# A retention layer and two MLPs: the split of w_out kept in DRAM, attention state in two tiles, and other warm-up matmuls

## The chip, the cores and the metric

The kernel runs on one core of a Trainium2 chip. The metric is the device time of one execution in microseconds, from its start to its end on that core. The profiled execution is one more run, taken with the hardware profiler; the span is the time from its first to its last instruction.

## The reference

Retention attention (a causal mask that decays with distance) over 8 sequences of 576 positions with 8 heads of 64, then two MLPs on the 4608 tokens. Activations are float32, the four weights are float64.

```python
Dmat = np.where(rel >= 0, gamma[:, None, None] ** rel[None, :, :], 0.0)
ret = scale * np.matmul(q, k.transpose(0, 1, 3, 2)) * Dmat[None]
x = np.matmul(ret, v)                     # 4608 tokens x 512
h = x @ moe_w_in                          # 512 x 2048
x = (h * (1.0 / (1.0 + np.exp(-1.702 * h)))) @ moe_w_out
h = x @ moe2_w_in
out = (h - np.tanh(h)) @ moe2_w_out
```

## The kernel before

**Tiles and steps.** The 4608 tokens are nine blocks of 512, the 2048 hidden units 16 slices f of 128. The main loop runs over steps s = (j, f), 288 in all: j = 0 to 8 are the nine blocks of the first MLP (MLP1), j = 9 to 17 the same blocks for the second (MLP2). A step has 12 matmuls of `mm_in(s)` (hidden slice f from `xh`, `xl` and `wi`) and 12 of `mm_out(s - 2)` (the slice of two steps before goes through `wos` into the four accumulators `acc`). Every float32 operand is split into a high part (rounded to fp32r, an ACT copy) and a low part (the rest, a subtraction), and three of the four products are summed; that makes 12 matmuls out of 4.

**Between the two products.** `act_a(s)` makes the nonlinearity. In MLP1 it is a tanh on ACT (L382) and one DVE operation (L383). In MLP2 it is tanh, square and another square on ACT (L387 to L389), then on DVE L390, L392, L393, L394 (a comparison that writes the mask) and L395 (the masked copy of a polynomial for small values). `act_b(s)`, which stands at the front of the next step, splits the result: `g` high on ACT (L400), `g` low on DVE (L401).

**w_out.** `wo` lies in SBUF as float32, one tile of 256 KB per f. In every step `split_wo` makes the two parts anew: ACT copies the high one (L187), POOL subtracts for the low one (L188). It stands behind `act_a(s)` in the code and works for `mm_out(s - 1)`, one step ahead of its use. For the second MLP the decoded `w_out` goes to DRAM (L134) and comes back in block j=8.

**w_in.** It is split once, when it is decoded: `wi` stays in SBUF. The second MLP's goes to DRAM (`w2s`, written from POOL's queue at L148) and is loaded back in j=8, also from POOL's queue.

**The decoder.** The float64 weights come in 64 chunks of 512 KB (`stg`, L93). A chunk takes DVE operations L103, L106, L111 and L117, an ACT operation (L105) and a multiplication on POOL (L126), in three pieces; `dec_c` then splits it (L142, L143). `dec_slot` runs three pieces: twice per step in j=0, and in every third step of j = 1 to 7.

**Attention.** 72 batches (36 tiles of 128 positions, two halves bt of the heads), one in every second step of j < 8. It makes the input of the MLP1 block one block ahead. `sbd` and `s_sb` hold the running state of all heads in one tile each; PE reads `sbd` at L246, DVE updates `s_sb` at L297. The loads of a tile (`at`, 1 MB, L207) wait for PE's last use of the buffer.

**MLP2's input.** The first MLP's result goes to DRAM block by block and comes back as `x2s`; `x2_split` copies its high part on ACT (L446) and subtracts for the low one on POOL (L447), in steps f = 6, 8, 10 and 12.

**Start.** Before the first attention batch stand 22 matmuls on zeros (L488). The order on each engine is the order of the code: scheduling is by hand, and each engine takes its instructions one after the other. DMAs that SP issues form one queue, those of POOL another.

Of the kernel before, what the change touches and what calls it, by code (L numbers as in the profile page):

```python
# [36 lines left out]
CA = C1 / (2 * C2)  # L37
CB = C0 / C2 - CA * CA
S_MAX = 0.0625
N_WARM = 22  # L40


@with_exitstack
def kernel(
# [32 lines left out]
    gt_sb = const.tile([P, HP], F32, name="gt_sb")  # L77
    ebias = const.tile([P, 1], F32, name="ebias")
    abias = const.tile([P, 1], F32, name="abias")
    sbd = const.tile([P, HP, P], F32, name="sbd")  # L80
    s_sb = const.tile([P, HP, HD], F32, name="s_sb")


    win = {}
    wout = {}
    w2_d = {}
    wo2_d = {}
    stg = {}
    half = {}

# [24 lines left out]
    def dec_b(m, f, c):  # L115
        hi, _, e, z = half[m, f, c]
        nc.vector.scalar_tensor_tensor(  # L117
            out=e, in0=hi, scalar=-(2 ** 31), in1=e, op0=ALU.bitwise_and, op1=ALU.bitwise_or
        )
        del stg[m, f, c]  # L120
        if c == 1 and m == 0:
            o = wts.tile([P, DM], F32, tag=f"wo{f}", name="wo")
            wout[f] = o
        else:
            o = z.bitcast(F32)
        nc.gpsimd.tensor_tensor(out=o, in0=z.bitcast(F32), in1=e.bitcast(F32), op=ALU.mult)  # L126
        half[m, f, c] = o

    def dec_c(m, f, c):
        o = half.pop((m, f, c))  # L130
        if c == 1:
            if m == 1:
                d = dram.tile([P, DM], F32, tag=f"wo2{f}", name="wo2")
                nc.sync.dma_start(out=d, in_=o)  # L134
                wo2_d[f] = d
            return
        if m == 0:
            s = wts.tile([P, 2, KD, P], F32R, tag=f"wi{f}", name="wi")
        else:
            s = st_p.tile([P, 2, KD, P], F32R, tag="stg", name="w2s", bufs=3)  # L140
        sv = s.rearrange("p a k c -> p a (k c)")
        nc.scalar.activation(out=sv[:, 0], in_=o, func=ACTF.Copy)  # L142
        nc.gpsimd.tensor_tensor(out=sv[:, 1], in0=o, in1=sv[:, 0].bitcast(F32), op=ALU.subtract)  # L143
        if m == 0:
            win[f] = s
        else:
            d = dram.tile([P, 2, KD, P], F32R, tag=f"w2{f}", name="w2")
            nc.gpsimd.dma_start(out=d, in_=s)  # L148
            w2_d[f] = d


    chunks = []
# [26 lines left out]
        for _ in range(3):  # L179
            dec_piece()  # L180

    wos = {}

    def split_wo(s):
        j, f = divmod(s, NF)
        t = t_p.tile([P, 2, DM], F32R, tag="wos", name="wos")
        nc.scalar.activation(out=t[:, 0], in_=wout[f], func=ACTF.Copy)  # L187
        nc.gpsimd.tensor_tensor(out=t[:, 1], in0=wout[f], in1=t[:, 0].bitcast(F32), op=ALU.subtract)  # L188
        wos[s] = t


    at = {}
# [42 lines left out]
    def result_of(ps):  # L235
        return ps[:, 1, 2 * P:4 * P].rearrange("p (k c) -> p k c", k=2)

    def bat_sq(b):

        t, bt = divmod(b, BPT)  # L240
        if t % TPS == 0:
            return False
        n = HD if t % TPS == 4 else P
        for k in range(2):
            hp = 2 * bt + k
            nc.tensor.matmul(  # L246
                result_of(pa[b])[:, k, 0:n], lhsT=sbd[:, hp], rhs=at[t][:, 0, hp * P:hp * P + n],
                start=k == 0, stop=False, skip_group_check=True,
            )
        return True  # L250
# [29 lines left out]
    def bat_p(b):  # L280
        t, bt = divmod(b, BPT)
        ps, p = pa[b], pt[b]
        nc.vector.tensor_tensor(
            out=p.rearrange("p i k c -> p i (k c)"), in0=ps[:, :, 0:2 * P],
            in1=mt_sb[:, bt].rearrange("p i k c -> p i (k c)"), op=ALU.mult,
        )
        if t % TPS == 4:
            nc.vector.memset(p[0:HD, :, :, HD:P], 0.0)
        if t % TPS == TPS - 1:
            return  # L290
        state = state_of(ps)
        if t % TPS in (0, 4):
            nc.vector.tensor_copy(out=s_sb[:, 2 * bt:2 * bt + 2], in_=state)
            return
        for k in range(2):
            hp = 2 * bt + k
            nc.vector.scalar_tensor_tensor(  # L297
                out=s_sb[:, hp], in0=s_sb[:, hp], scalar=gt_sb[:, hp:hp + 1], in1=state[:, k],
                op0=ALU.mult, op1=ALU.add,
            )  # L300

# [14 lines left out]
    def bat_x(b):  # L316
        t, bt = divmod(b, BPT)
        j, tl = divmod(t, TPB)
        x = result_of(pa.pop(b))
        if b % BPB == 0:  # L320
            xh[j] = x_p.tile([P, KD, BLK], F32R, tag="xh", name="xh")
            xl[j] = x_p.tile([P, KD, BLK], F32R, tag="xl", name="xl")
        c = slice(tl * P, (tl + 1) * P)
        hps_ = slice(2 * bt, 2 * bt + 2)
        nc.scalar.activation(out=xh[j][:, hps_, c], in_=x, func=ACTF.Copy)  # L325
        nc.vector.tensor_tensor(  # L326
            out=xl[j][:, hps_, c], in0=x, in1=xh[j][:, hps_, c].bitcast(F32), op=ALU.subtract
        )
        if t % TPS == TPS - 1:
            return  # L330
        for i in range(2):
            r = halves(i)
            nc.scalar.activation(out=sbd[r, hps_, r], in_=s_sb[r, hps_], func=ACTF.Copy)

    def attn_step(b, ps=None):

# [117 lines left out]
    def w2_load_out(f):  # L454
        t = wts.tile([P, DM], F32, tag=f"wo{f}", name="wo")
        nc.sync.dma_start(out=t, in_=wo2_d[f])
        wout[f] = t
# [12 lines left out]
    nc.vector.memset(sbd, 0.0)  # L470
# [28 lines left out]
    n_steps = 2 * NB * NF  # L499
    for s in range(n_steps + LAG):  # L500
        j, f = divmod(s, NF)
        so = s - LAG + 1
        if s >= n_steps and so < n_steps:
            split_wo(so)
        if 0 < s <= n_steps:
            act_b(s - 1)
        if j == 0:
# [78 lines left out]
```

## Time and profile before

| | us |
|---|---|
| median of three runs | 1818.05 |
| lowest and highest run | 1816.42, 1819.49 |
| the profiled execution | 1820.6 |
| its span | 1818.8 |

| engine | busy us | share of the span |
|---|---|---|
| PE (matmuls) | 1760.5 | 97% |
| PEld (weight loads) | 1428.1 | 79% |
| DVE | 1252.0 | 69% |
| ACT | 838.3 | 46% |
| POOL | 672.0 | 37% |

The mean granted clock of TensorE is 0.986 of the full one. The shares are averages over stages that differ: the start with the first nine attention batches (to 41.47 us), block j=0 with the densest decoding (to about 206), the other blocks of MLP1 with attention (to 916.72), block j=8 without attention (to 1003.76), and MLP2. The timeline names an instruction by start, duration, engine, line, tile written and tiles read; a bracket at its end tells how long the engine was idle before it and what it waited for. PEld is the weight load of a matmul. A group of several like instructions in a row is one line with their count.

### The profile page before, as it was taken

What the parts mean: (1) busy time and instruction counts of PE and PEld (TensorE: products, weight loads), DVE (VectorE), ACT (ScalarE), POOL (GpSimd) and SP (SyncE); (2) the same over time, 40 slices, a digit from 0 to 9 for tenths busy, and PEclk for the clock granted to TensorE, in tenths of its full rate; (3) what the DMA queues carried; (4) which work ended last, traced back from release to release, by engine and by line L of the source; (5) the groups of instructions that cost most, each with busy time, mean ns of one, the idle gap of its engine ahead of it and who ended that gap; (6) DMA issues with size and microseconds to landing.
All of it is one profiled execution on the core that took longest, in us unless ns stands there. A gap on an engine that the chain in (4) does not pass through costs nothing.

```text
span 1818.8 us, 22935 instructions
## 1 busy us (share of the span) xinstructions
PE 1760.5 (97%) x8918; PEld 1428.1 (79%) x8918; DVE 1252.0 (69%) x1689; ACT 838.3 (46%) x1555; POOL 672.0 (37%) x527
## 2 busy tenths in 40 slices
PE   7788899999999999999999999999999999999998
PEld 5556788888888888888888878787878787878787
DVE  6999756566565565633333687888887878788877
ACT  2444434334343434434333555555555555555554
POOL 4666544434344344432234232323232323232322
PEclk7999999999999999999999999999999999999999
DMA  5344323123222322211044201010101010101000
GB/s 216 117 138 151 133 87 103 72 99 125 90 98 88 122 87 95 86 53 70 1 145 143 84 1 47 1 47 1 47 1 47 1 47 1 46 1 47 1 23 24
DMA packets 36254, 126.61 MB, mean 70 GB/s; under 512 B 4400, under 2 KB 4528, under 8 KB 30512
## 3 DMA queue, kind: packets, MB, share of 16 engines
q1 hardware_dynamic: 30960, 108.28, 17.2%
q0 software_dynamic: 4608, 16.78, 2.6%
q8 instruction: 70, 1.15, 0.3%
q14 instruction: 40, 0.33, 0.1%
q10 hardware_dynamic: 576, 0.08, 0.0%
HBM read 93.67 MB, written 31.46 MB: 69 GB/s over the span
## 4 chain that ended last, share of the span: by engine, by line
PE 46%; DVE 32%; ACT 19%; issue 2%; POOL 1%; DMA 0%; SPq 0%; DVEq 0%; POOLq 0%; ACTq 0%
PE acc L414 20%; PE h L373 19%; DVE t L395 8%; DVE sq L394 6%; ACT pl L389 6%; DVE pl L392 6%; DVE pl L393 5%; ACT g L400 5%; ACT sq L388 4%; ACT t L387 4%; DVE z L106 2%; PE pat L260 2%; PE pat L311 1%; DVE e L117 1%; DVE g L401 1%
## 5 line engine op out<-in xcount | busy, mean ns | idle before, releaser
L373 PE MATMUL h<-xh,wi 128*128 128x512 f32 x2304 | 762.4, 392 | 11.2 <-POOL wi L143 6.1
L188 POOL TENSOR_TENSOR wos<-wo,wos 128x512 fp32r<-128x512 f32 x288 | 373.2, 1296 | 1034.8 <-ACT wos L187 1025.9
L373 PEld LDWEIGHTS h<-xh,wi 128*128 128x128 f32 x2304 | 434.6, 189 | 109.0 <-POOL wi L143 10.1
L414 PE MATMUL acc<-g,wos 128*128 128x512 f32 x1728 | 434.7, 400 | 20.4 <-ACT wos L187 11.5
L373 PE MATMUL h<-xl,wi 128*128 128x512 f32 x1152 | 450.3, 391 | 0.0
L416 PE MATMUL acc<-wos,g 128*128 128x512 f32 x1728 | 424.7, 392 | 12.1 <-POOL wos L188 12.1
L401 DVE TENSOR_TENSOR g<-t,g 128x512 fp32r<-128x512 f32 x288 | 289.3, 1005 | 194.8 <-ACT g L400 189.2
L414 PEld LDWEIGHTS acc<-g,wos 128*128 128x128 f32 x1728 | 324.1, 191 | 102.0 <-ACT wos L187 14.5
L416 PEld LDWEIGHTS acc<-wos,g 128*128 128x128 f32 x1728 | 321.7, 188 | 91.9 <-POOL wos L188 24.5
L400 ACT ACTIVATE g<-t 128x512 fp32r<-128x512 f32 x288 | 181.3, 630 | 388.3 <-DVE t L395 353.8
L373 PEld LDWEIGHTS h<-xl,wi 128*128 128x128 f32 x1152 | 217.5, 189 | 45.0
L383 DVE SCALAR_TENSOR_TENSOR t<-t,h 128x512 f32<-128x512 f32 x144 | 98.2, 682 | 139.6 <-ACT t L382 139.3
L187 ACT ACTIVATE wos<-wo 128x512 fp32r<-128x512 f32 x288 | 178.9, 621 | 1.6 <-PE acc L416 0.3
L382 ACT ACTIVATE t<-h 128x512 f32<-128x512 f32 x144 | 85.8, 596 | 162.7 <-PE h L373 161.4
L395 DVE COPY_PREDICATED t<-sq,pl 128x512 f32<-128x512 int32 x144 | 141.0, 979 | 5.0
L390 DVE TENSOR_TENSOR t<-h,t 128x512 f32<-128x512 f32 x144 | 99.7, 692 | 44.0 <-ACT sq L388 44.0
L325 ACT ACTIVATE xh<-pat 128x256 fp32r<-128x256 f32 x64 | 24.5, 382 | 225.2 <-PE pat L311 225.2
L326 DVE TENSOR_TENSOR xl<-pat,xh 128x256 fp32r<-128x256 f32 x64 | 27.0, 422 | 145.6 <-ACT xh L325 145.6
L394 DVE TENSOR_SCALAR sq<-sq 128x512 int32<-128x512 f32 x144 | 116.6, 810 | 0.0
L389 ACT ACTIVATE pl<-sq,abias 128x512 f32<-128x512 f32 x144 | 104.4, 725 | 4.7
L392 DVE SCALAR_TENSOR_TENSOR pl<-pl,sq 128x512 f32<-128x512 f32 x144 | 99.7, 693 | 9.5
L393 DVE SCALAR_TENSOR_TENSOR pl<-pl,h 128x512 f32<-128x512 f32 x144 | 98.9, 687 | 4.9
(61 smaller groups left out, 1286.0 us busy)
## 6 DMA issues: line engine op xcount, KB each, us to landing
at<-in_attn_dram SPq DMA_DIRECT2D x35, 1024.0 KB, 5.5
stg<-in_w_dram SPq DMA_DIRECT2D x64, 512.0 KB, 4.3
x<-o SPq DMA_DIRECT2D x36, 256.0 KB, 2.7
x2s<-x SPq DMA_DIRECT2D x9, 1024.0 KB, 5.5
out_dram<-o SPq DMA_DIRECT2D x36, 256.0 KB, 2.2
w<-w2s POOLq DMA_DIRECT2D x16, 512.0 KB, 3.1
wi<-w POOLq DMA_DIRECT2D x16, 512.0 KB, 4.1
wo<-z SPq DMA_DIRECT2D x16, 256.0 KB, 5.7
```

The lines of the kernel that those rows point to most:

```text
L187: nc.scalar.activation(out=t[:, 0], in_=wout[f], func=ACTF.Copy)
L188: nc.gpsimd.tensor_tensor(out=t[:, 1], in0=wout[f], in1=t[:, 0].bitcast(F32), op=ALU.subtract)
L373: nc.tensor.matmul(h, lhsT=win[f][:, a, k], rhs=xs[b][:, k], start=(n == 0), stop=(n == 3 * KD - 1))
L389: nc.scalar.activation(out=pl, in_=sq, func=ACTF.Square, bias=abias)
L392: nc.vector.scalar_tensor_tensor(out=pl, in0=pl, scalar=CB, in1=sq, op0=ALU.add, op1=ALU.mult)
L393: nc.vector.scalar_tensor_tensor(out=pl, in0=pl, scalar=C2, in1=h, op0=ALU.mult, op1=ALU.mult)
L394: nc.vector.tensor_scalar(sq.bitcast(I32), sq, S_MAX, None, ALU.is_lt)
L395: nc.vector.copy_predicated(out=t, mask=sq.bitcast(I32), data=pl)
L400: nc.scalar.activation(out=g[:, 0], in_=t, func=ACTF.Copy)
L401: nc.vector.tensor_tensor(out=g[:, 1], in0=t, in1=g[:, 0].bitcast(F32), op=ALU.subtract)
L414: nc.tensor.matmul(acc[m], lhsT=wo[:, a, c], rhs=g[:, b], start=first, stop=last)
L416: nc.tensor.matmul(acc[m], lhsT=g[:, a, c], rhs=wo[:, b], start=first, stop=last)
```

## The change

**w_out.** `split_wo` is gone. `dec_c` splits a decoded `w_out` chunk as it splits `w_in`: an ACT copy (L139 of the new file) and a POOL subtraction (L140) into a tile with both parts, 512 KB, which is written to DRAM (`wd`, L143) from SP's queue. In j=0 the same tile serves `mm_out` directly. From j=1 on `wo_load(s)` (L180) loads the two parts from DRAM in every step, on SP's queue, for use two steps later; the pool `wos` has four buffers. The float32 `wo` tiles, their write to DRAM for the second MLP and the 16 loads in j=8 go.

**w_in of the second MLP.** Its write and its loads move from POOL's queue to SP's.

**sbd, s_sb.** One tile per bt instead of one for both.

**Warm-up.** 12 matmuls of 512 columns in bf16 and 12 of 256 columns in fp32r on four weight slices, in place of 22 of 256 columns in bf16. A second zero tile is set on POOL.

```diff
-N_WARM = 22
+N_WARM = 12
...
+    wos_p = ctx.enter_context(tc.tile_pool(name="wos", bufs=4))
...
-    sbd = const.tile([P, HP, P], F32, name="sbd")
-    s_sb = const.tile([P, HP, HD], F32, name="s_sb")
+    sbd = [const.tile([P, 2, P], F32, name=f"sbd{bt}") for bt in range(BPT)]
+    s_sb = [const.tile([P, 2, HD], F32, name=f"s_sb{bt}") for bt in range(BPT)]
...
-        if c == 1 and m == 0:
-            o = wts.tile([P, DM], F32, tag=f"wo{f}", name="wo")
-            wout[f] = o
-        else:
-            o = z.bitcast(F32)
+        o = z.bitcast(F32)
...
         if c == 1:
-            if m == 1:
-                d = dram.tile([P, DM], F32, tag=f"wo2{f}", name="wo2")
-                nc.sync.dma_start(out=d, in_=o)
-                wo2_d[f] = d
-            return
-        if m == 0:
+            if m == 0:
+                s = wos[f] = wos_p.tile([P, 2, DM], F32R, tag="wos", name="wos")
+            else:
+                s = st_p.tile([P, 2, DM], F32R, tag="stg", name="w2s", bufs=3)
+        elif m == 0:
             s = wts.tile([P, 2, KD, P], F32R, tag=f"wi{f}", name="wi")
+            win[f] = s
         else:
             s = st_p.tile([P, 2, KD, P], F32R, tag="stg", name="w2s", bufs=3)
-        sv = s.rearrange("p a k c -> p a (k c)")
+        sv = s if c == 1 else s.rearrange("p a k c -> p a (k c)")
         nc.scalar.activation(out=sv[:, 0], in_=o, func=ACTF.Copy)
         nc.gpsimd.tensor_tensor(out=sv[:, 1], in0=o, in1=sv[:, 0].bitcast(F32), op=ALU.subtract)
-        if m == 0:
-            win[f] = s
-        else:
-            d = dram.tile([P, 2, KD, P], F32R, tag=f"w2{f}", name="w2")
-            nc.gpsimd.dma_start(out=d, in_=s)
-            w2_d[f] = d
+        if c == 1 or m == 1:
+            d = dram.tile([P, 2 * DM], F32, tag=f"w{m}{f}{c}", name="wd")
+            nc.sync.dma_start(out=d, in_=sv.rearrange("p a n -> p (a n)").bitcast(F32))
+            (wo_d if c else w2_d)[m, f] = d
...
-    def split_wo(s):
+    def wo_load(s):
         j, f = divmod(s, NF)
-        t = t_p.tile([P, 2, DM], F32R, tag="wos", name="wos")
-        nc.scalar.activation(out=t[:, 0], in_=wout[f], func=ACTF.Copy)
-        nc.gpsimd.tensor_tensor(out=t[:, 1], in0=wout[f], in1=t[:, 0].bitcast(F32), op=ALU.subtract)
-        wos[s] = t
+        t = wos[s] = wos_p.tile([P, 2, DM], F32R, tag="wos", name="wos")
+        nc.sync.dma_start(out=t.rearrange("p a n -> p (a n)").bitcast(F32), in_=wo_d[int(j >= NB), f])
...
-    def w2_load_in(f):
+    def w2_load(f):
         t = wts.tile([P, 2, KD, P], F32R, tag=f"wi{f}", name="wi")
-        nc.gpsimd.dma_start(out=t, in_=w2_d[f])
+        nc.sync.dma_start(out=t.rearrange("p a k c -> p (a k c)").bitcast(F32), in_=w2_d[1, f])
         win[f] = t
...
+        warm_r = g_p.tile([P, BLK], F32R, tag="g", name="warm_r")
+        nc.gpsimd.memset(warm_r.bitcast(F32), 0.0)
...
                     nc.tensor.matmul(
-                        ps[:, 1, 2 * P:], lhsT=warm[:, 0:P], rhs=warm[:, 2 * P:], start=True, stop=True
+                        ps[:, 1], lhsT=warm[:, 0:P], rhs=warm, start=True, stop=True
+                    )
+                for n in range(N_WARM):
+                    c = slice(n % 4 * P, (n % 4 + 1) * P)
+                    nc.tensor.matmul(
+                        ps[:, 1, 0:2 * P], lhsT=warm_r[:, c], rhs=warm_r[:, 0:2 * P], start=True, stop=True
                     )
...
         if s < n_steps:
             act_a(s)
-            if so >= 0:
-                split_wo(so)
-                if so // NF == NB - 1:
-                    w2_load_out(so % NF)
+            if j:
+                wo_load(s)
```

In MLP2, around a step with x2_split, ACT's row before (L387 to L389 of before are L378 to L380 of after, L400 is L391, L446 is L437):

```order
L387 ACTIVATE t<-h 128x512
L388 ACTIVATE sq<-h 128x512
L389 ACTIVATE pl<-sq,abias 128x512
L187 ACTIVATE wos<-wo 128x512
L446 ACTIVATE xh<-x2s 128x512
L400 ACTIVATE g<-t 128x512
```

In the changed program the same place of ACT's row reads:

```order
L378 ACTIVATE t<-h 128x512
L379 ACTIVATE sq<-h 128x512
L380 ACTIVATE pl<-sq,abias 128x512
L437 ACTIVATE xh<-x2s 128x512
L391 ACTIVATE g<-t 128x512
```

The copy of `wos` is gone, and the copy of x2 follows the second square directly.

SP's queue in MLP1 around the end of a block, before (`x` is the block's result on its way to DRAM, L425 and L416; L207 and L198 are the attention loads, L93 and L94 the decoder's loads):

```order
L425 DMA x_4876<-o 128x512 x4
L93 DMA stg<-in_w_dram 128x512
L134 DMA wo_4891<-z 128x512
L207 DMA at<-in_attn_dram 128x2048
L93 DMA stg<-in_w_dram 128x512
```

The end of a block in the changed program's SP queue:

```order
L180 DMA wos<-wd 128x1024 x3
L416 DMA x_2419<-o 128x512 x4
L94 DMA stg<-in_w_dram 128x512
L143 DMA wd<-w2s 128x1024
L198 DMA at<-in_attn_dram 128x2048
L180 DMA wos<-wd 128x1024 x3
L94 DMA stg<-in_w_dram 128x512
L143 DMA wd<-w2s 128x1024
```

The loads of `wos` now stand between the attention and decoder loads, one per step, and a write of both parts stands behind a decoder load.

## Rows read from the trace of the kernel before

**Rows 1.** Windows by stage: length, busy (instructions) by engine, clock, DMA share, GB/s
```profile
41.47:189.01 147.54, 119.15 (x592) 87.55 (x593) 142.36 (x181) 60.36 (x114) 92.59 (x66) 0.91 0.41 136
205.93:916.72 710.79, 710.79 (x4141) 583.91 (x4140) 396.85 (x537) 279.58 (x552) 283.14 (x219) 1.00 0.25 87
916.72:1003.76 87.04, 87.04 (x385) 72.07 (x384) 26.60 (x33) 31.59 (x56) 35.54 (x36) 1.00 0.50 157
1003.76:1801.92 798.16, 786.94 (x3433) 641.82 (x3432) 636.12 (x855) 441.71 (x782) 229.97 (x176) 1.00 0.07 24
```

**Rows 2.** Waits of PE: us in total, times, longest
```profile
PE acc L416 <- POOL wos L188: 12.1, 24, 0.9
PE acc L414 <- ACT wos L187: 11.5, 7, 1.7
PE pe L246 <- DVE s_sb L297: 4.2, 5, 2.2
```

**Rows 3.** Timeline of ACT, DVE and POOL in MLP2: start, us, instruction [idle before]
```profile
1401.71 1.48 POOL L447 TENSOR_TENSOR xl<-x2s,xh 128x512 fp32r<-128x512 f32 x1
1402.07 1.73 DVE L395 COPY_PREDICATED t<-sq,pl 128x512 f32<-128x512 int32 x1
1403.84 0.63 ACT L400 ACTIVATE g<-t 128x512 fp32r<-128x512 f32 x1 [2.94 <-DVE t L395]
1406.80 1.29 POOL L188 TENSOR_TENSOR wos<-wo,wos 128x512 fp32r<-128x512 f32 x1 [3.61 <-ACT wos L187]
1407.56 0.81 DVE L394 TENSOR_SCALAR sq<-sq 128x512 int32<-128x512 f32 x1
1408.14 2.38 PEld L416 LDWEIGHTS acc<-wos,g 128*128 128x128 f32 x11 [0.30 <-POOL wos L188]
1408.40 0.76 DVE L395 COPY_PREDICATED t<-sq,pl 128x512 f32<-128x512 int32 x1
1409.20 0.63 ACT L400 ACTIVATE g<-t 128x512 fp32r<-128x512 f32 x1 [2.48 <-DVE t L395]
```

**Rows 4.** Groups by line: busy us, mean ns, idle before
```profile
L187 ACT ACTIVATE wos<-wo 128x512 fp32r<-128x512 f32 x288 | 178.9, 621 | 1.6 <-PE acc L416 0.3
L394 DVE TENSOR_SCALAR sq<-sq 128x512 int32<-128x512 f32 x144 | 116.6, 810 | 0.0
```

**Rows 5.** Timeline from the end of block j=0 into j=1
```profile
185.23 3.94 PE L414 MATMUL acc<-g,wos 128*128 128x512 f32 x10 [0.63 <-POOL wos L188]
193.85 0.42 DVE L106 TENSOR_SCALAR z<-stg 128x512 int32<-128x512 int32 x1
195.48 1.22 DVE L401 TENSOR_TENSOR g<-t,g 128x512 fp32r<-128x512 f32 x1 [0.48 <-ACT g L400]
202.03 4.07 PE L414 MATMUL acc<-g,wos 128*128 128x512 f32 x10 [2.34 <-POOL wos L188]
205.93 0.40 PE L373 MATMUL h<-xh,wi 128*128 128x512 f32 x1
```

**Rows 6.** Timeline of the last steps
```profile
1808.74 3.45 PE L416 MATMUL acc<-wos,g 128*128 128x512 f32 x13 [0.86 <-POOL wos L188]
```

**Rows 7.** DMA issues in 45–200 and 200–900: KB, median us to landing
```profile
at<-in_attn_dram SPq DMA_DIRECT2D x4, 1024.0 KB, 6.4
stg<-in_w_dram SPq DMA_DIRECT2D x28, 512.0 KB, 5.8
```

**Rows 8.** Timeline and windows of the start
```profile
1.32 4.87 PE L488 MATMUL pe<-warm 128*128 128x256 bf16 x22 [1.32 <-POOL warm L474]
13.24 0.84 PE L275 MATMUL pe<-at 128*64 128x64 f32 x8 [1.60 <-POOL at L221]
...
10.70:17.60 6.90, 5.26 (x48) 3.95 (x48) 5.08 (x10) 1.85 (x4) 5.11 (x6) 0.51 0.99 416
17.60:27.80 10.20, 6.45 (x84) 5.08 (x84) 8.99 (x20) 5.84 (x15) 3.72 (x4) 1.00 0.43 152
27.80:44.90 17.10, 14.91 (x92) 11.78 (x93) 11.95 (x23) 4.96 (x12) 7.56 (x6) 0.50 0.35 129
```

More of the change, by code (lines that the diff above doesn't have):

```diff
@@ L79 @@
     abias = const.tile([P, 1], F32, name="abias")
-    sbd = const.tile([P, HP, P], F32, name="sbd")
-    s_sb = const.tile([P, HP, HD], F32, name="s_sb")
+    sbd = [const.tile([P, 2, P], F32, name=f"sbd{bt}") for bt in range(BPT)]
+    s_sb = [const.tile([P, 2, HD], F32, name=f"s_sb{bt}") for bt in range(BPT)]
     win = {}
-    wout = {}
+    wos = {}
     w2_d = {}
-    wo2_d = {}
+    wo_d = {}
     stg = {}
@@ L180, in dec_slot @@
             dec_piece()
-    wos = {}
-    def split_wo(s):
+    def wo_load(s):
         j, f = divmod(s, NF)
-        t = t_p.tile([P, 2, DM], F32R, tag="wos", name="wos")
-        nc.scalar.activation(out=t[:, 0], in_=wout[f], func=ACTF.Copy)
-        nc.gpsimd.tensor_tensor(out=t[:, 1], in0=wout[f], in1=t[:, 0].bitcast(F32), op=ALU.subtract)
-        wos[s] = t
+        t = wos[s] = wos_p.tile([P, 2, DM], F32R, tag="wos", name="wos")
+        nc.sync.dma_start(out=t.rearrange("p a n -> p (a n)").bitcast(F32), in_=wo_d[int(j >= NB), f])
     at = {}
@@ L246, in bat_sq @@
             nc.tensor.matmul(
-                result_of(pa[b])[:, k, 0:n], lhsT=sbd[:, hp], rhs=at[t][:, 0, hp * P:hp * P + n],
+                result_of(pa[b])[:, k, 0:n], lhsT=sbd[bt][:, k], rhs=at[t][:, 0, hp * P:hp * P + n],
                 start=k == 0, stop=False, skip_group_check=True,
@@ L292, in bat_p @@
         if t % TPS in (0, 4):
-            nc.vector.tensor_copy(out=s_sb[:, 2 * bt:2 * bt + 2], in_=state)
+            nc.vector.tensor_copy(out=s_sb[bt], in_=state)
             return
@@ L297, in bat_p @@
             nc.vector.scalar_tensor_tensor(
-                out=s_sb[:, hp], in0=s_sb[:, hp], scalar=gt_sb[:, hp:hp + 1], in1=state[:, k],
+                out=s_sb[bt][:, k], in0=s_sb[bt][:, k], scalar=gt_sb[:, hp:hp + 1], in1=state[:, k],
                 op0=ALU.mult, op1=ALU.add,
@@ L332, in bat_x @@
             r = halves(i)
-            nc.scalar.activation(out=sbd[r, hps_, r], in_=s_sb[r, hps_], func=ACTF.Copy)
+            nc.scalar.activation(out=sbd[bt][r, :, r], in_=s_sb[bt][r], func=ACTF.Copy)
     def attn_step(b, ps=None):
@@ L447, in x2_split @@
         nc.gpsimd.tensor_tensor(out=lo[:, k], in0=t[:, k], in1=hi[:, k].bitcast(F32), op=ALU.subtract)
-    def w2_load_in(f):
+    def w2_load(f):
         t = wts.tile([P, 2, KD, P], F32R, tag=f"wi{f}", name="wi")
-        nc.gpsimd.dma_start(out=t, in_=w2_d[f])
+        nc.sync.dma_start(out=t.rearrange("p a k c -> p (a k c)").bitcast(F32), in_=w2_d[1, f])
         win[f] = t
[L454 to L457, printed above, removed]
     nc.sync.dma_start(out=qt_sb, in_=qtab)
@@ L469 @@
     nc.vector.memset(abias, CA)
-    nc.vector.memset(sbd, 0.0)
+    for bt in range(BPT):
+        nc.vector.memset(sbd[bt], 0.0)
     with tc.tile_pool(name="ps_e", bufs=3, space=bass.MemoryType.PSUM) as ps_e:
@@ L501 @@
         j, f = divmod(s, NF)
-        so = s - LAG + 1
-        if s >= n_steps and so < n_steps:
-            split_wo(so)
         if 0 < s <= n_steps:
@@ L514 @@
             act_a(s)
-            if so >= 0:
-                split_wo(so)
-                if so // NF == NB - 1:
-                    w2_load_out(so % NF)
+            if j:
+                wo_load(s)
         if s >= LAG:
@@ L530 @@
         if j == NB - 1:
-            w2_load_in(f)
+            w2_load(f)
 def _layout(inputs):
```

## The prediction

> **What bounds the kernel now.** I read the windows by stage first [rows 1], since the share over the whole span mixes four stages with different limits. They show TensorE (PE) busy for all of 205.93–916.72 and 916.72–1003.76. The second stretch is sixteen steps without attention in 87.04 us, so a step of 24 matmuls costs **5.44 us** when nothing is waited for. The rest of MLP1 stands at that floor too, with attention on top, so whatever ACT, POOL and the DMA queues do there is covered, and work taken from them there is worth nothing. Two stages are above the floor. MLP2, 1003.76–1801.92, holds 143 steps in 798.16 us; at the floor they would take 143 × 5.44 = 777.9, so **20.2 us** are lost. Block j=0 (41.47–189.01) has VectorE busy for 142.36 of 147.54 us: it is bound by the decode on DVE.
>
> Next the waits, for what PE waits for [rows 2]: in MLP2 for POOL's `wos` of L188 and for nothing else that counts, in the first blocks for the ACT half of the same tile. The 12.1 us listed are less than 20.2, because part of a late step shows as a late weight load, as at 1408.14 [rows 3].
>
> Last the timeline of two steps of MLP2 [rows 3], to see why `wos` is late although its source is long in SBUF. It isn't POOL's speed: L188 alone is 1.3 us. ACT and DVE run one loop: `g` (L400) waits for DVE's L395, and the tanh and squares of the next step stand behind it, then DVE's five operations. The loop's period is 1409.20 − 1403.84 = 5.36 us in a plain step, just below the floor. In a step with an x2_split, POOL's L447 starts during L394 and L395 then takes 1.73 instead of 0.76 us, so the period is 5.36 + 0.97 = 6.3. With four such steps a block takes 12 × 5.36 + 4 × 6.3 = 89.5 us, against 87.04 for PE. The split of `w_out` hangs at the end of this loop (ACT's L187 behind the tanh chain, POOL's L188 behind that), so mm_out waits for it.
>
> **The change part by part.** *The split made once.* It takes 272 of the 288 L187 (0.62 us each, 169 us of ACT [rows 4]) and as many L188 (1.29 each, 351 us of POOL) out of steps 16 to 287, and adds 16 of each for the second `w_out` during MLP1, where PE covers them. What counts is the loop in MLP2:
> - PE no longer waits for the end of the loop through `wos`; mm_out(s-2) then needs only `g`, which the loop makes one step before.
> - The loop gets shorter. L394 takes 0.81 us in the mean of its 144 [rows 4]; in rows 3 it starts 0.53 before an L188 ends. L395 shows what is left of a DVE operation after such an overlap: L447 ends 1.12 us into it, and 0.61 follow, against 0.76 when free, so about 0.15 of it passes during the wait. For L394, 0.28 follow, so some 0.43 free; the free L106, also a tensor_scalar, takes 0.42 [rows 5]. The plain period becomes 5.36 − 0.39 = 4.97.
> - In a step with x2_split, L446 moves into L187's place and L447 into L188's. It starts 0.76 before L394 and lasts 1.48, so L394 ends 0.72 + 0.28 = 1.00 after its start, 0.19 later than now, and L395 is free: 5.55. A block is 12 × 4.97 + 4 × 5.55 = 81.8 us, below PE's 87.04.
>
> PE is the limit again and **20.2 us** go. The other end, if 0.81 is L394's own length: an x2_split step has 0.72 + 0.66 in its place and comes to 5.93, a block to 12 × 5.36 + 4 × 5.93 = 88.0, (88.0 − 87.04) × 143/16 = 8.6 us of the excess stay, and 11.6 go. I take 20.2, since two kinds of rows give 0.42. The Trainium skill's "SBUF — State Buffer", section "Terms", says that VectorE and GpSimd arbitrate for one port pair, that the lock is held for a full instruction and that the loser blocks fully; L395 with 0.76 and 1.73 agrees, and by it the sum would be the same 20.2.
>
> *The tail.* mm_out(286) waits 0.86 us for POOL's L188 [rows 6]: **0.9 us** go.
>
> *The end of j=0.* There ACT and POOL do as much as before (the split in the decoder replaces the one in the step), and DVE's stream, which bounds the block, has the same instructions: 0. But `wos` is made one step earlier, and after the last decode PE catches up. Now mm_out(13) waits at 185.23 and spreads over 3.94 us, and mm_out(15) waits at 202.03 for L188, runs ten matmuls at the lower clock level and ends at 205.93 [rows 5]. After, mm_out(15) is bound by `g`'s low part, 195.48 + 1.22 = 196.70, and eleven matmuls of 5.44 / 24 = 0.227: 199.2. That is 6.7 us; I take **6.5**, with ends at 2.3 (the last wait alone) and 8.
>
> *DMA.* SP gets 272 loads of 512 KB, 96 GB/s in a 5.44 us step, and 32 writes; w2's writes and the `wi` loads move to it from POOL's queue. In 916.72–1003.76 the engines moved 157 GB/s at a share of 0.50, with PE 100% busy, against 87 and 0.25 in 205.93–916.72 [rows 1]. The new sum lies near what has been covered. Lateness: in MLP1 the worst load stands behind an attention load that waits for PE's pv inside step s; mm_out(s) comes two steps later. Attention costs 2.0 us in every second step (110 steps, 55 with it, in the 710.79 us), so there are 2.72 + 5.44 + 2.72 + 2.0 = 12.9 us. The landings of both together are 6.4 + 5.8 = 12.2 [rows 7], though each of these already holds time behind others. I take 0; the other end is the third rival.
>
> *sbd and s_sb per batch.* In the built order the same instructions wait for the same ones, so I take 0. Between the ends 0 and 4.2 (all PE waits for `s_sb` go [rows 2]) 0 is the nearer. One more memset on DVE lies in the first microseconds, before PE has its data.
>
> *Warm-ups.* 22 matmuls of 256 columns took 4.87 us [rows 8], so twelve of 512 take 5.3. The fp32r ones of 256 columns have no row; by the floor's 0.227 for 512 columns at the full clock, 0.11 to 0.23 each. They end near 9.3 instead of 6.2. Then qk(0) and qk(1) follow, and state(1) at 13.24, which waits for POOL today, still does. Ends: +3.1 (all of it delays), and −6.1 (first rival). Taken: 0.
>
> **Sum.** 20.2 + 0.9 + 6.5 = 27.6 us. The profiled execution took 1820.6 us with a span of 1818.8, and would come to 1793.0. It lies 2.55 above the median of 1818.05, so the median becomes **1790.4 us**.
>
> **The rivals.**
> 1. *The clock of the start.* The granted clock was 0.51 in 10.70–17.60 and 0.50 in 27.80–44.90, the 1.2 GHz level [rows 8]. If the longer warm-ups, which leave PE no pause before qk(0), keep the 2.4 GHz level: the first window holds 5.26 us of PE and gains 2.6; in the second DVE's 11.95, at the 88% that it has in 17.60–27.80, need 13.6 instead of 17.1, so 3.5. Time: 1784. Against: 17.60–27.80 ran at the full clock with PE busy 63%, and the clock fell after it all the same.
> 2. *The loop still bounds MLP2*, because L394 needs 0.81 by itself or POOL's L447 hits another operation: 11.6 in place of 20.2, so 1799, and up to 1804 with some delay from the warm-ups. For: no row shows an L394 without L188.
> 3. *Slower: the wait moves to SP.* All transfers now stand in one queue in order, with attention loads in it that wait for PE. If a `wos` load behind one of them lands later than 12.9 us from its turn, PE waits in MLP1, where today it never does. There are 28 such places (every fourth of 112 steps); 1 us late at each, a landing at 13.9, eats the 27.6, and 2 us late, 56 us, makes 1846. For it: the margin between 12.2 and 12.9 is thin. Against: 6.4 and 5.8 already hold time that these transfers spent behind others. The Trainium skill's "DMA: Bandwidth & Descriptors", section "Queues, rings and completion order", says that a DMA engine takes turns between queue rows; by it the moved loads lose a turn of their own against SP's, as in this rival. No row here shows a load delayed for that.
> 4. *It doesn't do what it says*: another producer ends as late as `wos` did (a late `g`, say), and PE's excess stays: 1818. Against: in MLP2 PE waits for `wos` and not for `g` [rows 2].
>
> **How the numbers follow.** Forecast 0.60 (1786 to 1796); first rival 0.10; second 0.15; third 0.08; fourth 0.04; the last 0.03 lie between 1804 and 1814. The range 1783 to 1804 takes in the first three, 0.85. Against 1818.05, with 0.2% (3.6 us) as about what a measurement of this kernel can tell from no change: faster 0.88, same 0.04, slower 0.08.
>
> **What would show it.** In the profile after: MLP2's blocks at 87 us with PE 100% busy and no wait for `wos`; L394 near 0.42 in plain steps and near 1.0 in four of sixteen; L395 0.76 throughout; mm_in(18), at 205.93 now, near 199; MLP1 still without PE waits, the mean clock near 0.986. Wrong it would be by a PE wait for a `wos` load (third rival), by L394 at 0.81 without POOL (second), or by a start shorter than 38 us or longer than 43 (warm-ups).

## The result and the profile after

The changed kernel takes **1791.55 us** (median of four runs, 1789.62 to 1794.65), against 1817.34 for the kernel before in the same comparison: a ratio of 0.9858, with an interval from 0.9840 to 0.9876. The prediction was 1790.4 us, in a range from 1783 to 1804; of the 27.6 us that it took off, 25.8 are there by these medians. The profiled execution has a span of 1792.9 us, 25.9 below 1818.8.

The first part of the page of the changed kernel, with busy time and share of the span for each engine:

```profile
PE 1749.3 (98%) x8920; PEld 1430.8 (80%) x8920; DVE 1076.5 (60%) x1690; ACT 717.9 (40%) x1299; POOL 329.4 (18%) x240
```

POOL's work has halved, which by itself says nothing about the time. The windows by stage of the changed kernel do (columns as in [rows 1]; the stages are the start, block j=0 up to mm_in(18), the rest of MLP1 with attention, block j=8, MLP2 up to its last mm_in, the tail):

```profile
0.00:41.99 41.99, 30.66 (x256) 22.38 (x256) 26.03 (x61) 11.33 (x29) 16.17 (x21) 0.76 0.59 221
41.99:201.88 159.89, 131.60 (x661) 99.87 (x662) 153.37 (x194) 66.78 (x126) 102.83 (x73) 0.89 0.57 186
201.88:912.60 710.72, 710.72 (x4141) 583.69 (x4140) 303.58 (x539) 230.08 (x460) 163.91 (x111) 1.00 0.49 176
912.60:999.70 87.10, 87.10 (x386) 72.10 (x385) 23.44 (x33) 24.06 (x40) 5.17 (x4) 1.00 0.61 210
999.70:1777.60 777.90, 777.90 (x3434) 644.12 (x3433) 562.35 (x855) 381.35 (x639) 41.37 (x32) 1.00 0.35 121
1777.60:1792.90 15.30, 11.32 (x49) 8.66 (x47) 7.75 (x13) 4.27 (x7) 0.00 (x0) 1.00 0.18 69
```

The fifth row answers to the last of [rows 1]: 143 steps take 777.90 us instead of 798.16, with PE busy in all of them. That is the floor, and **20.26 us** of the 25.9. MLP1 stays where it was (710.72 against 710.79), although the DMA engines now move 176 instead of 87 GB/s there. mm_in(18), PE's first work behind the last mm_out of block j=0, comes at 201.84 instead of 205.93, **4.1 us** earlier, and the tail takes 15.30 instead of 16.88 (1818.8 less 1801.92), **1.6 us** less. The three make up the 25.9.

Two steps of MLP2 in the timeline of the changed kernel, a plain one and one with x2_split (L385, L386 and L391 are L394, L395 and L400 of before, L438 is L447):

```profile
1381.16 0.42 DVE L385 TENSOR_SCALAR sq<-sq 128x512 int32<-128x512 f32 x1
1381.61 0.76 DVE L386 COPY_PREDICATED t<-sq,pl 128x512 f32<-128x512 int32 x1
1382.40 0.63 ACT L391 ACTIVATE g<-t 128x512 fp32r<-128x512 f32 x1 [2.61 <-DVE t L386]
...
1385.83 1.30 POOL L438 TENSOR_TENSOR xl<-x2s,xh 128x512 fp32r<-128x512 f32 x1 [53.11 <-ACT xh L437]
1386.60 0.82 DVE L385 TENSOR_SCALAR sq<-sq 128x512 int32<-128x512 f32 x1
1387.45 0.76 DVE L386 COPY_PREDICATED t<-sq,pl 128x512 f32<-128x512 int32 x1
```

The comparison (L385) takes 0.42 us when POOL is idle and 0.82 when it starts 0.53 before a POOL operation ends. The masked copy (L386) takes 0.76 in both. In [rows 3] these were 0.81, and 0.76 or 1.73. What the loop waits for now stands in the waits of the changed kernel (us in total, times, longest):

```profile
ACT t L378 <- PE h L364: 42.8, 111, 3.7
```

ACT waits for PE's result in 111 of 144 steps: the loop has become the faster of the two.

### The profile page after: what moved, and what is told of

Read it like the earlier page. It is cut to its first block, busy times and chain, and to the rows that moved or that the text cites. A ratio compares the mean times of both kernels' runs of the same rounds, so it can differ in the third digit from the quotient of the medians.

```text
span 1792.9 us, 22946 instructions
## 1 busy us (share of the span) xinstructions
PE 1749.3 (98%) x8920; PEld 1430.8 (80%) x8920; DVE 1076.5 (60%) x1690; ACT 717.9 (40%) x1299; POOL 329.4 (18%) x240
## 4 chain that ended last, share of the span: by engine, by line
PE 90%; DVE 8%; issue 1%; DMA 0%; ACT 0%; POOL 0%; SPq 0%; DVEq 0%; POOLq 0%
PE h L364 41%; PE acc L407 22%; PE acc L405 20%; DVE z L107 2%; PE pat L251 2%; DVE g L392 2%; PE pat L302 1%; DVE e L118 1%; PE pat L237 1%; PE pat L266 1%; DVE e L104 1%; DVE t L374 1%; DMA at<-in_attn_dram 0%; DVE z L112 0%; DVE p L274 0%
## 5 line engine op out<-in xcount | busy, mean ns | idle before, releaser
L405 PE MATMUL acc<-g,wos 128*128 128x512 f32 x1728 | 424.1, 394 | 0.6 <-DVE g L392 0.5
L407 PE MATMUL acc<-wos,g 128*128 128x512 f32 x1728 | 415.0, 389 | 0.0
L405 PEld LDWEIGHTS acc<-g,wos 128*128 128x128 f32 x1728 | 319.4, 188 | 75.6 <-issue 9.4
L392 DVE TENSOR_TENSOR g<-t,g 128x512 fp32r<-128x512 f32 x288 | 238.3, 827 | 209.4 <-ACT g L391 209.4
L391 ACT ACTIVATE g<-t 128x512 fp32r<-128x512 f32 x288 | 181.3, 630 | 433.1 <-DVE t L386 354.4
L374 DVE SCALAR_TENSOR_TENSOR t<-t,h 128x512 f32<-128x512 f32 x144 | 98.3, 682 | 157.4 <-ACT t L373 156.9
L438 POOL TENSOR_TENSOR xl<-x2s,xh 128x512 fp32r<-128x512 f32 x36 | 46.5, 1293 | 774.2 <-ACT xh L437 774.2
L373 ACT ACTIVATE t<-h 128x512 f32<-128x512 f32 x144 | 86.0, 598 | 173.4 <-PE h L364 172.1
L140 POOL TENSOR_TENSOR w2s<-z,w2s 128x512 fp32r<-128x512 f32 x32 | 53.8, 1683 | 383.9 <-ACT w2s L139 383.9
L386 DVE COPY_PREDICATED t<-sq,pl 128x512 f32<-128x512 int32 x144 | 109.2, 759 | 4.9
L123 POOL TENSOR_TENSOR z<-z,e 128x512 f32<-128x512 f32 x64 | 100.1, 1564 | 35.3 <-DVE e L118 35.3
L380 ACT ACTIVATE pl<-sq,abias 128x512 f32<-128x512 f32 x144 | 104.1, 723 | 4.8
L378 ACT ACTIVATE t<-h 128x512 f32<-128x512 f32 x144 | 86.1, 598 | 42.8 <-PE h L364 42.8
```

The costliest lines, as they stand in the source:

```text
L374: nc.vector.scalar_tensor_tensor(out=t, in0=t, scalar=1.0, in1=h, op0=ALU.add, op1=ALU.mult)
L378: nc.scalar.activation(out=t, in_=h, func=ACTF.Tanh)
L380: nc.scalar.activation(out=pl, in_=sq, func=ACTF.Square, bias=abias)
L386: nc.vector.copy_predicated(out=t, mask=sq.bitcast(I32), data=pl)
L391: nc.scalar.activation(out=g[:, 0], in_=t, func=ACTF.Copy)
L392: nc.vector.tensor_tensor(out=g[:, 1], in0=t, in1=g[:, 0].bitcast(F32), op=ALU.subtract)
```

## The experiments

The kernel before ran between 1815 and 1823 us on the chips of these runs, so each is compared by its ratio to it; the changed kernel stands at 0.9858.

**Was it the loop, or the wait for the split?** Either would explain the gain. The first kernel gives the loop its old POOL operation back and leaves mm_out on the loaded parts; the second gives back ACT's copy alone (`dummy(False)`).

```diff
+    def dummy(pool):
+        d = t_p.tile([P, 2, DM], F32R, tag="dum", name="dum")
+        nc.scalar.activation(out=d[:, 0], in_=dsrc, func=ACTF.Copy)
+        if pool:
+            nc.gpsimd.tensor_tensor(out=d[:, 1], in0=dsrc, in1=d[:, 0].bitcast(F32), op=ALU.subtract)
...
             if j:
                 wo_load(s)
+            if j >= NB:
+                dummy(True)
```

> The changed kernel, with an ACT copy and a POOL subtraction of the old size put back at the old place (behind act_a) in every step of MLP2. They work on a constant tile and nobody reads their result; mm_out still uses the loaded parts. Theory A (the loop of ACT and DVE was the limit, and POOL's subtraction lengthens it): the comparison goes back from 0.42 to 0.81 us, the masked copy to 1.73 in the steps with x2_split, a block of MLP2 to about 89.5 us, and the time to 1810 to 1813 us, although PE no longer waits for any split. Theory B (the loss was that mm_out waited for the split, the loop was fast enough): MLP2 stays at 87.0 us a block and the time at 1791 to 1793.

> As the run before, with the ACT copy alone put back and no POOL subtraction. Theory A (POOL's lock lengthens the loop): the comparison stays at 0.42 us, blocks at 87.0, the time within 1 us of the changed kernel, 1791 to 1792. A rival, that it was ACT's 0.62 us at the end of its chain that made the loop long: blocks of 88 us or more and 1800 or later.

With POOL's subtraction: 1814.68 us, ratio 0.9978 (0.9968 to 0.9987), a little above the 1810 to 1813 of theory A and far from theory B. With the copy alone: 1793.42 us, 0.9858 (0.9841 to 0.9874), by the ratio where theory A had it. Its comparison keeps the 0.42 us in plain steps; the mean is 0.62 and not 0.42, because in the steps with x2_split POOL's operation starts just ahead of it and it takes 1.33. PE's time covers that. The groups by line of the first (mean ns of one behind the busy time; L392 is the comparison, L393 the masked copy) and the window of its block j=11:

```profile
L393 DVE COPY_PREDICATED t<-sq,pl 128x512 f32<-128x512 int32 x144 | 140.2, 973 | 4.9
L392 DVE TENSOR_SCALAR sq<-sq 128x512 int32<-128x512 f32 x144 | 117.1, 813 | 0.0
```
```profile
1175.70:1265.50 89.80, 88.09 (x386) 71.80 (x386) 72.00 (x97) 49.67 (x88) 26.51 (x21) 1.00 0.34 118
```

The block is back at 89.8 us, with means of 0.81 and 0.97 (0.81 and 0.98 in the kernel before), and all of MLP2's gain is gone, though nobody waits for the subtraction. So the loss was the length of the loop, and mm_out's wait for `wos` in [rows 2] was only where it became visible. Without that wait PE finds most of the same lateness elsewhere, once a block:

```profile
PE acc L414 <- ACT o L430: 12.3, 8, 1.7
```

That row is from the waits of the first kernel: PE waits for the accumulators, which ACT empties between two blocks. That ACT is late there because its copy stands behind the loop in its order is read from the code, not tried.

**Where is the gain?** Only the second MLP's `w_out` is split once and loaded; but for where the tiles of `w_out` lie, everything else is the kernel before.

```diff
-            if so >= 0:
+            if 0 <= so < NB * NF:
                 split_wo(so)
-                if so // NF == NB - 1:
-                    w2_load_out(so % NF)
+            if j >= NB:
+                wo_load(s)
```

> The kernel before, with only the second MLP's w_out split once and loaded in every step of MLP2; MLP1 splits in every step as before, and warm-ups, state tiles and the decoder's order are those of before. If the gain is MLP2 and the tail alone there: 20.2 + 1.6 = 21.8 us go, 1795.5 us, 4 us later than the changed kernel, which also has 4.1 us from the end of block j=0. If the work taken from ACT and POOL in MLP1 is worth something besides: slower than 1798.

Measured: 1798.03 us, ratio 0.9880 (0.9865 to 0.9894). The bare time would stand at the rival's 1798, but the kernel before ran 2 us longer beside it, at 1819.3; by the ratio it is 4.0 us above the changed kernel, as expected. The profiled span is 1796.9, 21.9 below 1818.8 and 4.0 above the changed kernel; MLP2's blocks take 87.0 us, mm_in(18) stands at 205.6. From there to the end it takes 1591.3 us, the changed kernel 1591.1. So behind block j=0 the 112 steps of MLP1 freed of their splits, the moved transfers of `w_in` and the divided `sbd` and `s_sb` are together worth nothing, as predicted.

**How near is the queue to its edge?** One and two more loads of 512 KB per step stand ahead of each load (`range(2)` in the second kernel).

```diff
     def wo_load(s):
         j, f = divmod(s, NF)
+        for _ in range(1):
+            d = t_p.tile([P, 2 * DM], F32, tag="dum", name="dum")
+            nc.sync.dma_start(out=d, in_=wo_d[int(j >= NB), f])
```

> The changed kernel with a second load of the same 512 KB, into a tile that nobody reads, ahead of every load of the split w_out on SP's queue. In the changed kernel MLP1 moves 176 GB/s at a DMA share of 0.49; with 96 GB/s more the share becomes about 0.76. Theory (the loads have a lead of 12.9 us and room beside them): no wait of PE for a load, the time within 1.5 us of the changed kernel (ratio to before 0.985 to 0.987). Rival (the queue was at its edge, 12.2 of 12.9 us): PE waits in MLP1 in the steps after an attention load, 28 times 1 us or more, so 28 us or more above the changed kernel.

> As the run before with two added loads per step: MLP1's DMA share by the same reckoning is 1.03, MLP2's 0.35 * 313 / 121 = 0.91. Theory: MLP1 is at the edge of what the DMA engines move, with waits of PE for loads there and 5 to 40 us lost in it, MLP2 still at 87.0 us a block. Rival of the run before: both stages wait, over 60 us lost.

One more: 1794.85 us, ratio 0.9860 (0.9845 to 0.9874). Two more: 1813.17, 0.9980 (0.9959 to 1.0002). The windows of MLP1 (205 to 908 us) of the two kernels, in this order:

```profile
205.00:908.00 703.00, 703.00 (x4087) 577.17 (x4086) 301.28 (x536) 226.89 (x456) 162.59 (x110) 1.00 0.69 259
```
```profile
205.00:908.00 703.00, 689.56 (x4002) 564.25 (x4001) 294.50 (x527) 221.18 (x445) 162.36 (x110) 1.00 0.93 335
```

At 259 GB/s and a DMA share of 0.69 PE is never idle. At 335 and 0.93 it is, for 13.4 us, and most of its waits name the loads. The wait of PE over the whole run, and the longest one of SP's queue between 205 and 908 us:

```profile
PE acc L408 <- DMA wos<-wd: 10.3, 9, 2.9
SPq L181 <- DMA dum<-wd: 385.5, 179, 8.1
```

So the queue of the changed kernel has room for another 83 GB/s (259 against 176). With two more loads MLP1 loses most of what MLP2 gained, within the 5 to 40 us of that run's theory. Late loads are what the third rival feared, but what makes them late is open: SP itself waited 385.5 us for the buffers of the added loads, which exist twice, and the run doesn't tell that from the share of 0.93 or from the attention loads in the queue.

**The warm-ups.** The changed kernel with those of before:

```diff
-N_WARM = 12
+N_WARM = 22
...
-                        ps[:, 1], lhsT=warm[:, 0:P], rhs=warm, start=True, stop=True
-                    )
-                for n in range(N_WARM):
...
+                        ps[:, 1, 2 * P:], lhsT=warm[:, 0:P], rhs=warm[:, 2 * P:], start=True, stop=True
+                    )
```

> The changed kernel with the warm-up matmuls of the kernel before. The start took 41.5 us before and 42.0 after. If the new warm-ups only move the stretches at the lower clock: within 1.5 us of the changed kernel, either sign, with the lower clock again at 10.7 to 17.6 and 27.8 to 44.9. If they cost what the start lost: 0.5 us faster. If they help block j=0: 2 us or more slower.

Measured: 1793.69 us, ratio 0.9858 (0.9843 to 0.9873): no difference. The lower clock did not come where it was expected: at 10.7 to 17.6 the granted clock was 0.50 again, but 0.83 and 0.70 in the two windows behind it, where [rows 8] has 1.00 and 0.50:

```profile
17.60:27.80 10.20, 7.92 (x84) 6.27 (x84) 8.01 (x16) 4.74 (x13) 3.68 (x3) 0.83 0.35 116
27.80:44.90 17.10, 12.45 (x93) 9.79 (x94) 12.95 (x25) 5.55 (x14) 7.92 (x6) 0.70 0.41 151
```

The first mm_in stands at 41.2 us, against 42.0 in the changed kernel. With the same warm-ups as that one, it stands at 42.3 in e1_split_back, at 39.7 in e2_copy_back and at 38.6 in e5_load_2x, so what one execution's start shows is less than executions differ.

**What made the end of j=0 gain 4.1 us and not 6.5?** DVE's decoder came 2.4 us later at its end than before, 0.5 of it from the start and 1.9 from the block. In what follows "the block" is the time from mm_in(0) to mm_in(16): 147.5 us before, 144.5 in the changed kernel. The split of `wos` is made a step earlier, so I put it back behind act_a, from a float32 tile, in two versions: with the write to DRAM at once (in `split_wo`, without the last two lines), and with the write behind the step's loads.

```diff
+            if 0 < s <= NF:
+                split_wo(s - 1)
             if j:
                 wo_load(s)
...
             dec_slot()
+        if 0 < s <= NF:
+            wo_store(s - 1)
```

> The changed kernel, with the split of the first MLP's w_out in block j=0 put back to where the old one stood, behind act_a one step later, from a float32 tile with four buffers. If the 1.9 us that DVE's stream lost in j=0 came from POOL's subtraction one step earlier: the decoder's operations run with the old kernel's offsets, the block from the first matmul to mm_in(18) takes 158 instead of 159.9 us, and the time is 1 to 2 us below the changed kernel (ratio to before 0.9845 to 0.985). Rival: the split is late for mm_out again, and the 4.6 us gained there go back: 2 to 4 us above it.

> As e6_late_split, with one thing moved: the write of the split to DRAM stands on SP's queue behind the decoder's loads of the step, not ahead of them. In e6_late_split SP waited 124 us in block j=0 for POOL's subtraction with that write, the loads stood behind it, and the block took 160.6 us. Theory (the queue in order made the loads late): no wait of DVE for the decoder's loads, the block back at 143 to 147.5 us, ratio to before 0.984 to 0.987. Rival (the late split itself costs it, by waits of PE for it): the block stays over 155 us, ratio 0.992 or more.

Measured: e6_late_split 1808.84 us, ratio 0.9943 (0.9931 to 0.9955); e6b_late_store 1795.58, 0.9867 (0.9851 to 0.9883). The first missed both of its theories; the second came out as its theory had it, but for the block's 148.1 us instead of at most 147.5. In e6 the block takes 160.6 us; the write waits on SP for POOL, and the decoder's loads stand behind it. Two waits of DVE and SP in e6 (42 to 200 us):

```profile
DVE e L105 <- DMA stg<-in_w_dram: 6.7, 12, 1.1
SPq L187 <- POOL wos L185: 124.2, 14, 9.5
```

With the write behind the loads DVE's wait for them is gone, and 12.5 us of the block with it; DVE's own waits are 6.7 of them, the rest isn't divided up. So one queue in order did cost time, in another place than my third rival had put it. From the first mm_in to mm_in(18), e6b takes 164.7 us, the kernel before 164.5 and the changed one 159.8: the early split gives some 4.6 us there, net of what DVE's stream loses. The times of the two kernels, 0.9867 and 0.9858, lie within their intervals. PE's waits of e6b name the split again, as in [rows 2], and its last `g` of the block has this row:

```profile
PE acc L421 <- ACT wos L184: 11.4, 7, 1.8
194.35 1.22 DVE L408 TENSOR_TENSOR g<-t,g 128x512 fp32r<-128x512 f32 x1 [0.48 <-ACT g L407]
```

The guess behind e6 has two halves. The first holds: that `g` starts 154.4 us behind the first mm_in (39.98 in e6b), against 154.0 in the kernel before ([rows 5]) and 155.9 in the changed one, so the early split is what costs DVE's stream most of its 1.9 us. The second, that the time would gain by a later split, fell, since PE then waits for the split.

**Can DVE's waits for POOL in block j=0 be avoided?** First by order: the piece with L118 and the POOL operations ahead of attention.

```diff
+        if j == 0:
+            dec_piece()
         if j < NB - 1 and s % 2 == 0:
             attn_step(s // 2 + BPB + 1)
...
-        if j == 0 or (j < NB - 1 and s % 3 == 0):
+        if j == 0:
+            dec_piece()
+            dec_piece()
+        elif j < NB - 1 and s % 3 == 0:
             dec_slot()
```

> The changed kernel, with the first piece of the second decode slot of a step in block j=0 (DVE's L118, the POOL multiplication behind it, the split two chunks before) moved ahead of attention and act_a. DVE then has operations on PSUM (L317, L274, L288, L374) to do while POOL multiplies, where it now has L104 and L107 on SBUF, of which L107 takes 1.5 instead of 0.42 us. If POOL's lock is what makes block j=0 long: 1.08 us less in each of 8 steps with attention and some 0.5 in the 8 others, 8 to 13 us below the changed kernel (ratio to before 0.979 to 0.982). If PE or the hand-offs between the engines bind it: within 3 us of it or slower.

Measured: 1799.98 us, ratio 0.9890 (0.9878 to 0.9903), slower than the changed kernel; the block takes 149.6 us. The groups by line of DVE between 60 and 180 us, of e7_order and then of the changed kernel:

```profile
L118 DVE SCALAR_TENSOR_TENSOR e<-stg,e 128x512 int32<-128x512 int32 x24 | 42.7, 1778 | 0.0
L107 DVE TENSOR_SCALAR z<-stg 128x512 int32<-128x512 int32 x24 | 24.7, 1031 | 0.0
L392 DVE TENSOR_TENSOR g<-t,g 128x512 fp32r<-128x512 f32 x12 | 8.3, 690 | 2.5 <-ACT g L391 2.5
```
```profile
L107 DVE TENSOR_SCALAR z<-stg 128x512 int32<-128x512 int32 x25 | 37.7, 1507 | 0.0
L392 DVE TENSOR_TENSOR g<-t,g 128x512 fp32r<-128x512 f32 x12 | 21.2, 1769 | 0.0
L118 DVE SCALAR_TENSOR_TENSOR e<-stg,e 128x512 int32<-128x512 int32 x25 | 21.0, 840 | 0.0
```

L107 and L392 became cheaper, L118 dearer by about as much: the wait went to whichever operation on SBUF came next, while those that read PSUM keep their length (L374 0.67 and 0.68 us, L274 0.67 and 0.68). So the time came out as the rival had it, but not by its cause, PE or the hand-offs; where the 5 us more come from was not tried. DVE is idle for 3.3 of these 120 us instead of 0.9, and L104 takes 0.67 instead of 0.41. Then by engine: the multiplication alone, and multiplication and subtraction, of the first MLP's chunks on DVE. The second of the two (with the lines about `dec_rest`, which makes the subtraction) has it behind the slot's last piece.

```diff
-        nc.gpsimd.tensor_tensor(out=o, in0=z.bitcast(F32), in1=e.bitcast(F32), op=ALU.mult)
+        eng = nc.vector if m == 0 else nc.gpsimd
+        eng.tensor_tensor(out=o, in0=z.bitcast(F32), in1=e.bitcast(F32), op=ALU.mult)
...
+        rest.append((m, f, c, o, s, sv))
+        if m:
+            dec_rest()
...
+        if k == 2:
+            dec_rest()
```

> The changed kernel, with the decoder's multiplication for the first MLP's 32 chunks (line 123) on DVE instead of POOL. In block j=0 POOL's two operations a chunk each make one DVE operation 1.08 us longer (L107 1.51 instead of 0.42, L392 1.77 instead of 0.69); on DVE one takes 0.69. Theory (DVE pays more for POOL's work than it would for doing it): some 0.4 us less a chunk, 10 to 14 us below the changed kernel, ratio 0.978 to 0.981. Rival (the wait only moves to the next DVE operation, and DVE's own 0.6 come on top): 10 to 19 us slower than the changed kernel, ratio 0.991 or more.

> As e9a_mult_dve, with the subtraction for the low part of these chunks on DVE too, after the slot's other operations. Theory: no POOL operation of the decoder is left in block j=0, the DVE operations take 0.42 and 0.69 us, the block falls to 120 to 130 us, 18 to 25 us below the changed kernel, ratio 0.972 to 0.976. Rival: DVE waits for ACT's copy ahead of each subtraction, since it takes its instructions in order, and the block stays at 140 us or more.

The multiplication alone: 1803.41 us, ratio 0.9910 (0.9895 to 0.9924), as the rival had it. Both: **1778.31 us**, 0.9774 (0.9758 to 0.9790), the fastest kernel here and about 15 us below the changed one by the ratios. That is less than the 18 to 25 of its theory. From the groups by line between 60 and 160 us, two of e9a and then two of e9b (L151 is the subtraction on DVE):

```profile
L118 DVE SCALAR_TENSOR_TENSOR e<-stg,e 128x512 int32<-128x512 int32 x20 | 35.4, 1772 | 0.0
L141 POOL TENSOR_TENSOR wos<-z,wos 128x512 fp32r<-128x512 f32 x10 | 12.8, 1276 | 37.1 <-ACT wos L140 37.1
```
```profile
L108 DVE TENSOR_SCALAR z<-stg 128x512 int32<-128x512 int32 x22 | 9.2, 420 | 0.0
L151 DVE TENSOR_TENSOR wos<-z,wos 128x512 fp32r<-128x512 f32 x11 | 7.5, 685 | 0.0
```

With one POOL operation a chunk left, it makes every L118 wait: 1.77 instead of 0.84 us. With none left the two operations shown run at 0.42 and 0.69 us, and the block takes 134.9 us, 9.7 less than in the changed kernel, longer than the 120 to 130 that I expected. DVE still has no room there: it is busy for 98.48 of the 100 us between 60 and 160, now with POOL's work on top. The profiled execution also reaches its first mm_in at 37.3; how much of that is the change, the spread of the starts above doesn't let one say.

## Why the prediction was right, point by point

The largest term was right in mechanism and size. The two small ones were off in opposite directions, the end of j=0 by 2.4 us too much and the tail by 0.7 too little, so it is partly luck that the sum, 27.6, came as near to 25.9. The fourth rival is out too: in MLP2 the waits of PE name no other producer.

- **The loop in MLP2** (20.2 predicted, 20.26 measured). Shown by the trace and by e1 and e2: the comparison takes 0.42 us when POOL is idle, as worked out from what was left of L395 after its wait and from L106. The second rival, that 0.81 was its own, is out. The x2_split step was priced too high, since the POOL operation takes 1.30 now and not the 1.48 of L447: L385 takes 0.82, not 1.00. It made no difference, as the loop lies below PE's time.
- **The tail** (0.9 predicted, 1.6 measured). The mechanism was right, the size not. I took only PE's wait in [rows 6]. The end is set by the last `g`: in the kernel before, the second of two L188 ran into the last L395, which took 1.73 us. In the changed kernel POOL is idle there and L386 takes 0.75. The row of before, then that of the changed kernel:

```profile
1809.00 1.73 DVE L395 COPY_PREDICATED t<-sq,pl 128x512 f32<-128x512 int32 x1
1784.17 0.75 DVE L386 COPY_PREDICATED t<-sq,pl 128x512 f32<-128x512 int32 x1
```

- **The end of j=0** (6.5 predicted, 4.1 measured). The step that was mis-sized is "DVE's stream has the same instructions: 0". mm_out(15) is bound by `g`'s low part, as predicted, but that comes 2.44 us later than in [rows 5]. The rows of the changed kernel:

```profile
50.90 2.68 POOL L140 TENSOR_TENSOR wos<-z,wos 128x512 fp32r<-128x512 f32 x1 [2.61 <-ACT wos L139]
54.06 1.74 DVE L392 TENSOR_TENSOR g<-t,g 128x512 fp32r<-128x512 f32 x1
56.33 1.49 DVE L104 TENSOR_SCALAR e<-stg 128x512 int32<-128x512 int32 x1
189.97 1.76 DVE L392 TENSOR_TENSOR g<-t,g 128x512 fp32r<-128x512 f32 x1
197.92 1.22 DVE L392 TENSOR_TENSOR g<-t,g 128x512 fp32r<-128x512 f32 x1 [0.48 <-ACT g L391]
199.19 2.81 PE L405 MATMUL acc<-g,wos 128*128 128x512 f32 x11 [0.46 <-DVE g L392]
```

  And in the kernel before, at the place of L104:

```profile
54.02 1.75 DVE L117 SCALAR_TENSOR_TENSOR e<-stg,e 128x512 int32<-128x512 int32 x1
55.70 0.41 DVE L103 TENSOR_SCALAR e<-stg 128x512 int32<-128x512 int32 x1
```

  The start gave 0.5 us away, less than executions of one start differ, so that part is chance. Near 51 us the first split, one step earlier than before, brings one more POOL operation. Three DVE operations close together now take over 1 us more than when free (the first `g`, L104, and L107 behind it with 1.53), where in the kernel before two did (L117, and L106 with 1.50). The decoder's offset goes from 0.6 to 1.7 us there and stays between 1.72 and 1.84 for 28 chunks. At 189.97 it happens again (0.68 before, 1.08 lost), and 0.5 come back at the end, where before a split was still to be made. Same instructions on DVE, but another partner on POOL; e6b, with the split late again, loses only 0.4.
- **DMA** (0 predicted, 0 measured). No wait of PE for a load; e5_load_2x shows room for another 83 GB/s. I had set the margin at 12.2 of 12.9 us by adding two landings, and that was too near: with a third transfer in between nothing is late. The place that the third rival named is there, in the waits of SP's queue from 205 to 908 us, in front of attention loads:

```profile
SPq L198 <- PE pat L302: 164.4, 23, 17.3
```

  Behind these waits no load of `wos` was late for PE. The moved transfers share one queue with the others now; no run shows that this costs anything. The Trainium skill's "DMA: Bandwidth & Descriptors", section "Queues, rings and completion order", has a DMA engine take turns between queue rows. No run here puts a number on that.
- **Warm-ups and start** (0 predicted; 0.5 later in this execution, which is less than executions differ). The warm-ups were priced too high: the twelve of 512 columns took 4.40 us and not 5.3, the fp32r ones 1.77, and they ended near 7.1 and not 9.3. The stretches at the lower clock moved and did not go. The windows of the changed kernel (the column before the last two is the granted clock):

```profile
11.50:25.10 13.60, 11.66 (x96) 9.32 (x96) 7.80 (x18) 3.49 (x10) 5.45 (x7) 0.50 0.51 203
25.10:35.40 10.30, 5.88 (x74) 4.53 (x72) 10.14 (x19) 4.73 (x12) 7.13 (x6) 1.00 0.76 292
35.40:45.60 10.20, 8.85 (x53) 6.87 (x54) 6.16 (x13) 3.35 (x8) 2.71 (x2) 0.50 0.15 48
```

  The first is longer than the one in [rows 8], the last shorter. The first rival is out: the lower level is still there in two stretches, and after one at the full clock with PE busy 57% the granted clock fell again.
- **sbd and s_sb** (0 predicted). PE's waits for `s_sb` are 5.2 us, against 4.2 before. That part was not tried alone; e4, without it, and e6b, with it, bound it, since they match the changed kernel behind mm_in(18) and the kernel before ahead of it.

## What to carry to other kernels

Where an engine waits for the last link of a chain, ask whether the chain's period or that link is late: taking the wait away while its work remains gives nothing, as e1 shows. A POOL operation beside DVE work on SBUF is priced by the DVE operation that it meets, about 1.1 us here, and moving it only chooses which one; if DVE is the limit, 0.69 us on DVE itself can be the cheaper place, here only once all of it had moved. On a queue in order, put a write that waits behind the loads that don't.

## What was not expected of the hardware

A DVE operation that waits for POOL doesn't pay its whole length afterwards: by the recorded ends, about 0.13 us pass during the wait (0.82 us with 0.53 of wait, 0.42 free; in e2_copy_back 1.33 with 1.05 of wait). The profile's spans on POOL are rough, so it may also be that POOL lets go that much before its recorded end. The Trainium skill's "SBUF — State Buffer", section "Who interferes with whom", says that the order of issue decides who blocks, and that the other blocks fully. The runs agree on the order (e7 and e9a moved the wait from L107 to L118, 0.84 to 1.78 us), and what they show differs from "fully" by these 0.13 us, if the recorded ends are right.
